# Moving work between the stages of a four-layer attention kernel: q of the linear layers, v of the second one, constants, and the order on each engine

## The chip, the cores and the metric

The kernel runs on one core of one Trainium2 chip. The profile lists its engines apart: TensorE (PE) for matrix products, with weight loads as PEld; VectorE (DVE); ScalarE (ACT); GpSimd (POOL); and SyncE (SP), which issues the DMAs here. They run side by side: before, PE, DVE, ACT and POOL are busy 445.8, 415.8, 389.4 and 59.1 us of one span of 532.9. The metric is device time in microseconds (us). The profile is one execution of the same program; its span is about 2 us shorter than the time of that execution (532.9 of 534.6 us before).

## The reference, cut to what matters

Four layers in a row on x of 2048 tokens by 512: linear attention (A), sliding-window attention (B), A again, B again, all with 32 heads of 16. The two A layers share weights, and so do the two B layers.

```
x = x + A(norm(x)); x = x + B(norm(x)); x = x + A(norm(x)); x = x + B(norm(x))

A:  q, k, v = x @ wqkv ;  phi(t) = where(t > 0, t + 1, exp(t)) + 1e-6
    kv = sum over all tokens of phi(k) v ;  z = sum over all tokens of phi(k)
    o = (phi(q) kv) / (phi(q) z + 1e-6) ;  o @ wo
B:  q, k, v = x @ wqkv ;  softmax(q k / 4) over the last 256 tokens ;  p v ;  o @ wo
```

Two things decide the shape of the program. In A, every output token needs `kv` and `z`, which need k and v of all tokens, so each A layer is a barrier. But q of a token is needed only when that token's output is made. In B the softmax needs one exp for each score in the window, a large fixed load for ACT (the 512 exps took it 305.9 us before).

Of the kernel before, what the change touches and what calls it, by code (L numbers as in the profile page):

```python
# [10 lines left out]
P = 128  # L11
D = 512
# [10 lines left out]
    cap_s=6, cap_d=2, cap_e=6, mode=100, sem=35, k_pv=0.669, k_wo=0.738, k_next=1.117, k_q=2.69, k_ao=4.2, k_kv=2.62, k_v=0.435, ring_x=3, pe_first=4, pe_last=1,  # L23
# [63 lines left out]
def schedule(g, par):  # L87
# [39 lines left out]
    while done < len(ops):  # L127
# [6 lines left out]
        while pending and pending[0][0] <= t:  # L134
            _, i = heapq.heappop(pending)
            for e in ops[i].engs:
                heapq.heappush(ready[e], (ops[i].key, i))
# [5 lines left out]
        for e in engines:  # L143
# [3 lines left out]
            pick = None  # L147
            while ready[e]:
# [8 lines left out]
                if need:  # L157
                    if any(used[c] + m > cap[c] for c, m in need.items()) or pick_banks(banks, held, need) is None:
                        back.append((k, i))
                        continue  # L160
                pick = o
# [125 lines left out]
class Plan:  # L287


    def __init__(self, par):  # L290
        self.par = par
        self.g = Graph()
        self.build()
# [27 lines left out]
    def setup(self):  # L321
# [30 lines left out]
        pool("c3", zero(lambda: K.bmask, 1.0), 1, 200, wr=[("bmask",)])  # L352
        pool("c4", lambda e: e.affine_select(out=K.bmask[:], in_=K.bmask[:], compare_op=ALU.is_ge, fill=0.0, base=0, pattern=[[-16, 8], [0, 16]], channel_multiplier=1), 2, 300, rd=[("bmask",)], wr=[("bmask",)])
        pool("c5", lambda e: e.affine_select(out=K.bmask[:], in_=K.bmask[:], compare_op=ALU.is_ge, fill=0.0, base=15, pattern=[[16, 8], [0, 16]], channel_multiplier=-1), 3, 300, rd=[("bmask",)], wr=[("bmask",)])

        pool("c6", zero(lambda: K.hot, 1.0), 4, 200, wr=[("hot",)])
        pool("c7", lambda e: e.affine_select(out=K.hot[:], in_=K.hot[:], compare_op=ALU.is_ge, fill=0.0, base=0, pattern=[[128, 4], [-16, 32]], channel_multiplier=1), 5, 300, rd=[("hot",)], wr=[("hot",)])
        pool("c8", lambda e: e.affine_select(out=K.hot[:], in_=K.hot[:], compare_op=ALU.is_ge, fill=0.0, base=15, pattern=[[-128, 4], [16, 32]], channel_multiplier=-1), 6, 300, rd=[("hot",)], wr=[("hot",)])
        pool("c9", zero(lambda: K.spread), 7, 2000, wr=[("spread",)])
        for tg in range(4):  # L360
            pool("c10", lambda e, tg=tg: e.affine_select(out=K.spread[:, tg, :, :], in_=K.spread[:, tg, :, :], compare_op=ALU.not_equal, fill=1.0, base=-32 * tg, pattern=[[-8, 4], [-1, 8], [0, 16]], channel_multiplier=1), 8, 700, rd=[("spread",)], wr=[("spread",)])
        pool("c11", zero(lambda: K.eps), 9, 100, wr=[("eps",)])
        pool("c12", lambda e: e.memset(K.eps[0:1, :], EPS_HI), 10, 100, rd=[("eps",)], wr=[("eps",)])
        pool("c13", lambda e: e.memset(K.eps[32:33, :], EPS_LO), 10, 100, rd=[("eps",)], wr=[("eps",)])

        pool("c14", zero(lambda: K.tri, 1.0), 11, 200, wr=[("tri",)])
        sel = lambda i, base, pat, cm: (lambda e: e.affine_select(out=K.tri[:, i, :], in_=K.tri[:, i, :], compare_op=ALU.is_ge, fill=0.0, base=base, pattern=pat, channel_multiplier=cm))
        pool("c15", sel(0, 0, [[1, 64]], -1), 12, 200, rd=[("tri",)], wr=[("tri",)])
        pool("c15", sel(1, 64, [[1, 64]], -1), 12, 200, rd=[("tri",)], wr=[("tri",)])
        pool("c15", sel(1, -64, [[0, 64]], 1), 12, 200, rd=[("tri",)], wr=[("tri",)])  # L370
# [3 lines left out]
        pool("c17", lambda e: e.iota(K.row[:], pattern=[[0, 1]], base=0, channel_multiplier=1), 13, 150, wr=[("row",)])  # L374
# [4 lines left out]
        for s in range(4):  # L379
            pool("c21", lambda e, s=s: e.memset(K.vB[:, s, :, :, :], 0.0), 17, 1100, wr=[("vB", s)])  # L380
            pool("c22", lambda e, s=s: e.memset(K.vB[0:64, s, :, :, 16:17], 1.0), 18, 130, rd=[("vB", s)], wr=[("vB", s)])
            pool("c23", lambda e, s=s: e.memset(K.vB[64:128, s, :, :, 33:34], 1.0), 18, 130, rd=[("vB", s)], wr=[("vB", s)])

        for q in range(2):
            for k in range(4):
                pool("wp", lambda e, q=q, k=k: e.tensor_copy(
                    K.wBp[:, q, k, :].rearrange("p (r a d) -> p r a d", a=2, d=DH),
                    K.nat(512 * q, 512 * q + 512)[:, k, :].rearrange("p (a r d) -> p r a d", a=2, d=DH)), 20 + q, 700,
                    rd=[("wBn",)], wr=[("wBp", q, k)])
        for s in range(3):  # L390
            pool("c24", lambda e, s=s: e.memset(K.pb[:, s, :, :, 320:384], 0.0), 30, 1000,
# [65 lines left out]
    def phi(self, ps, out, wr, key):  # L457
        K = self
        s = self.n_phi = getattr(self, "n_phi", -1) + 1
        s %= 3  # L460
# [4 lines left out]
    def a_k(self, t, key):  # L465
# [3 lines left out]
        self.phi(ps, lambda: K.pk[:, t, :], [("pk", t)], key + 0.1)  # L469
# [7 lines left out]
    def a_q(self, t, key):  # L477
        K = self
        ps = self.feat("q", t, lambda c, f: K.wA[:, c, f * P:(f + 1) * P], lambda c: K.XQ[:, c, t * P:(t + 1) * P], [("XQ", t), ("wAq",)], key)
        self.phi(ps, lambda: K.XQ[:, :, t * P:(t + 1) * P], [("XQ", t)], key + 0.1)  # L480

    def a_kv(self, t, kv, z, key):
# [12 lines left out]
        self.pe("kv", put, key, 4, 128, occ=330, rd=[("pk", t), ("vA", t), ("ones",)], ps=[kv, z])  # L495

    def layer_a_keys(self, ph, base):
        self.cls = "E"
        for t in range(T):
# [4 lines left out]
            self.a_q(t, k + 1.0)  # L504

    def barrier(self, ph):
# [3 lines left out]
        kv, z = Tile(1, "K", late), Tile(1, "K", late)  # L510
        key = 100 * ph + 16
        for t in range(T):
            self.a_kv(t, kv, z, key + 1.7 + t * 0.001 if late else 100 * ph + t + 0.6)
        key += 2
        if late:
            for t in range(T):
                self.a_q(t, key + t * 0.05)
# [321 lines left out]
```

## The kernel before: the parts that the change touches

The program is not written in its final order. Python code lists operations with a priority key (small is early), the engines that may do them, and what they read and write. A greedy list scheduler with estimated durations then fixes the order on each engine. At each moment an engine takes the ready operation with the smallest key whose PSUM banks are free. So a key is only a wish: an operation with a late key still runs early if its engine would otherwise idle.

```python
PAR = dict(cap_s=6, cap_d=2, cap_e=6, ..., k_pv=0.669, k_wo=0.738, k_next=1.117, k_q=2.69, k_ao=4.2, ...)

# the choice, once per engine and moment (cut)
while ready[e]:
    k, i = heapq.heappop(ready[e]); o = ops[i]
    ...
    if need:      # PSUM banks that this operation has to take first
        if any(used[c] + m > cap[c] for c, m in need.items()) or pick_banks(banks, held, need) is None:
            back.append((k, i))
            continue                     # and go on to the next key
    pick = o
    break
```

Constants (masks, selectors, zeros) are built by GpSimd with keys 1 to 30. The norms come at keys from 100, and their power `rs = (var + eps) ** -0.5` runs on GpSimd too.

```python
pool("c9", zero(lambda: K.spread), 7, 2000, wr=[("spread",)])     # one of some 40 like it
...
def layer_a_keys(self, ph, base):                # first A layer
    for t in range(T):                           # T = 16 tiles of 128 tokens
        k = 100 * ph + t
        self.norm(t, k - 0.5, ...)
        self.a_k(t, k)
        self.a_v(t, k + 0.05)
        self.a_q(t, k + 1.0)                     # q right behind k and v

def barrier(self, ph):                           # end of an A layer
    ...                                          # sums kv and z; if late (second A layer): key of a_kv is key + 1.7
    if late:
        for t in range(T):
            self.a_q(t, key + t * 0.05)          # all q of the second A layer, in plain order
    ...                                          # M = kv @ wo, denominators, reciprocals

def middle(self, ph):                            # a B layer, with A's output in front of it
    ...
    for j in range(T):                           # a "step": 8 score groups, 16 exps, 4 value groups
        ...                                      # front of tile j + 3: A's output, norm, B's q and k
        for f in range(4):
            for b in range(2):
                self.b_scores(j, f, b, base + j + (2 * f + b) / 8)
            ...                                  # b_values
        ...                                      # B's output, next norm
        self.a_k(j, k + 0.2)                     # second A layer's k and v of the same tile
        self.a_v(j, k + 0.3)
```

A score group is four matmuls into four PSUM banks, followed by two exps. A step has eight such groups.

The softmax here doesn't subtract the row's maximum and nothing guards it: scores larger than these inputs give would overflow.

## Time and profile before

The time before is 535.9 us (median of 4 runs, 534.8 to 537.3). I cut the span into stages at events that the trace shows: first matmul, last matmul of the first `kv` and `z`, first exp of the second layer, first exp of its twelfth step, its last exp, and first and last exp of the last layer.

| stage | before, us |
|---|---|
| start, to the first matmul | 21.6 |
| keys of the first A layer | 54.9 |
| first barrier, to the first exp | 22.2 |
| second layer, 11 steps | 138.7 |
| second layer, rest, to its last exp | 59.5 |
| second barrier, to the next first exp | 49.2 |
| last layer, first to last exp | 178.8 |
| end | 8.0 |

The windows view of the kernel before gives each engine's busy time (and instruction count) in roughly these stretches, then the granted PE clock, the DMA share and GB/s:

```profile
core 0: us, PE busy (x) PEld busy (x) DVE busy (x) ACT busy (x) POOL busy (x), PEclk, DMA share, GB/s
0.00:22.00 22.00, 0.44 (x4) 0.35 (x4) 7.79 (x31) 1.28 (x1) 18.45 (x44) 1.00 0.88 286
22.00:76.00 54.00, 52.64 (x566) 35.14 (x564) 42.12 (x102) 35.71 (x62) 13.69 (x23) 1.00 0.01 2
76.00:99.00 23.00, 16.79 (x258) 11.34 (x256) 18.79 (x38) 7.80 (x16) 2.19 (x4) 1.00 0.01 2
99.00:237.00 138.00, 126.51 (x1996) 77.21 (x1996) 123.53 (x300) 122.37 (x204) 11.47 (x21) 0.99 0.18 31
237.00:297.00 60.00, 52.37 (x869) 31.46 (x868) 42.36 (x113) 47.55 (x92) 3.38 (x7) 0.89 0.14 26
297.00:346.00 49.00, 42.05 (x667) 32.87 (x667) 37.59 (x81) 17.82 (x33) 2.91 (x6) 0.97 0.02 4
346.00:525.00 179.00, 151.82 (x2740) 99.84 (x2738) 142.01 (x326) 156.32 (x266) 6.97 (x12) 0.92 0.14 32
```

Read it by stage. In the start it is mostly GpSimd that works (18.45 of 22 us; DVE 7.79, PE 0.44). In the keys PE is busy 97% of the time. In the first eleven steps of the second layer PE, DVE and ACT all stand near 90% (126.51, 123.53 and 122.37 of 138 us), so no engine is "the" limit. In the last layer they stand at 85, 79 and 87%.

The timeline of GpSimd before shows why PE starts so late. The last constants run until 20.4, and `rs` only then. In the same trace DVE had the first `ve`, which `rs` reads, at 4.8 us:

```profile
17.85 0.52 POOL L382 MEMSET vB<- 64x32 bf16 x2
18.43 1.97 POOL L391 MEMSET pb<- 128x1024 bf16 x2
20.48 5.10 POOL L402 TENSOR_TENSOR rs<-ve,negh 128x1 f32<-128x1 f32 x8
```

So in this trace `rs`, with its input ready, waited some 15.7 us (20.48 less 4.8) behind constants that nobody needed yet.

### The profile page before, as it was taken

What the parts mean: (1) busy time and instruction counts of PE and PEld (TensorE: products, weight loads), DVE (VectorE), ACT (ScalarE), POOL (GpSimd) and SP (SyncE); (2) the same over time, 40 slices, a digit from 0 to 9 for tenths busy, and PEclk for the clock granted to TensorE, in tenths of its full rate; (3) what the DMA queues carried; (4) which work ended last, traced back from release to release, by engine and by line L of the source; (5) the groups of instructions that cost most, each with busy time, mean ns of one, the idle gap of its engine ahead of it and who ended that gap; (6) DMA issues with size and microseconds to landing.
All of it is one profiled execution on the core that took longest, in us unless ns stands there. A gap on an engine that the chain in (4) does not pass through costs nothing.

```text
span 532.9 us, 16311 instructions
## 1 busy us (share of the span) xinstructions
PE 445.8 (84%) x7124; PEld 289.6 (54%) x7124; DVE 415.8 (78%) x988; ACT 389.4 (73%) x673; POOL 59.1 (11%) x114
## 2 busy tenths in 40 slices
PE   0399987888999999999877997888998989787676
PEld 0156754644655556566444675655555656555443
DVE  4497769788988899999765759899799889777543
ACT  0166762689988889899886343389799889899962
POOL 8860001001000010000000000100000000000000
PEclk9999999989999999999887999899899999999756
DMA  8500000011221111121111000002121111121001
GB/s 276 197 2 1 2 2 2 1 31 31 32 33 31 32 31 32 33 35 38 32 22 21 12 1 2 1 12 42 25 47 31 33 42 33 32 50 33 21 22 31
DMA packets 45767, 18.48 MB, mean 35 GB/s; under 512 B 38016, under 2 KB 45184, under 8 KB 45696
## 3 DMA queue, kind: packets, MB, share of 16 engines
q1 hardware_dynamic: 45696, 17.44, 14.3%
q8 instruction: 56, 0.92, 0.7%
q14 instruction: 15, 0.12, 0.1%
HBM read 6.29 MB, written 2.10 MB: 16 GB/s over the span
## 4 chain that ended last, share of the span: by engine, by line
PE 45%; DVE 30%; ACT 14%; DMA 5%; POOL 4%; issue 2%; POOLq 0%; DVEq 0%
PE ps L438 14%; ACT pb L624 10%; PE ps L452 10%; PE ps L652 9%; DVE xres L565 5%; PE ps L612 5%; DVE pb L632 4%; PE ps L592 3%; DVE vB L427 3%; DVE kB L579 3%; DVE stats L399 3%; DMA oT<-o 3%; DMA XQ<-xn 2%; DVE pqd L559 2%; DVE XQ L463 2%
## 5 line engine op out<-in xcount | busy, mean ns | idle before, releaser
L624 ACT ACTIVATE pb<-ps 128x640 bf16<-128x640 f32 (+4 forms) x512 | 305.9, 675 | 33.1 <-PE ps L612 30.2
L632 DVE TENSOR_TENSOR pb<-pb,tri 128x512 bf16<-128x512 bf16 x224 | 92.7, 415 | 16.4 <-ACT pb L624 15.0
L612 PE MATMUL ps<-XQ,kB 32*128 32x320 bf16 (+4 forms) x1024 | 80.7, 305 | 26.5 <-ACT pb L624 24.9
L652 PE MATMUL ps<-vB,pb 128*128 128x34 bf16 x2880 | 90.6, 179 | 4.9 <-DVE xres L565 2.0
L652 PEld LDWEIGHTS ps<-vB,pb 128*128 128x128 bf16 x2880 | 80.8, 97 | 18.8 <-DVE xres L565 3.9
L402 POOL TENSOR_TENSOR rs<-ve,negh 128x1 f32<-128x1 f32 x64 | 35.9, 561 | 391.7 <-DVE ve L401 378.7
L612 PEld LDWEIGHTS ps<-XQ,kB 32*128 32x128 bf16 x1024 | 26.0, 91 | 86.1 <-ACT pb L624 70.7
L452 PE MATMUL ps<-xT,wBp 128*128 128x128 bf16 x1024 | 69.5, 221 | 3.0 <-DVE kB L579 0.9
L438 PE MATMUL ps<-wA,XQ 128*128 128x512 bf16 x256 | 67.0, 395 | 4.4 <-DMA XQ<-xn 2.8
L461 ACT ACTIVATE tE<-ps 128x512 bf16<-128x512 f32 x64 | 38.0, 597 | 37.7 <-PE ps L438 19.0
L452 PEld LDWEIGHTS ps<-xT,wBp 128*128 128x128 bf16 x1024 | 58.3, 98 | 12.2 <-DVE kB L579 1.2
L565 DVE TENSOR_TENSOR xres<-ps,xres 128x512 bf16<-128x512 f32 x64 | 43.8, 686 | 12.3 <-PE ps L438 11.8
L399 DVE BATCH_NORM_STATS2 stats<-xres 128x6 f32<-128x512 bf16 x64 | 43.1, 683 | 3.3 <-DMA xres<-in_A_x_dram 3.1
L579 DVE TENSOR_TENSOR kB<-ps,half 128x1024 bf16<-128x1024 f32 x32 | 39.1, 1221 | 6.8 <-PE ps L452 6.6
L438 PE MATMUL ps<-wBo,oT 128*128 128x512 bf16 x128 | 35.9, 402 | 6.6 <-DMA oT<-o 2.9
L438 PE MATMUL ps<-M,pqd 128*128 128x512 bf16 x128 | 36.0, 403 | 4.6 <-DVE pqd L559 2.7
L592 PE MATMUL ps<-wBv,xT 128*64 128x256 bf16 x512 | 37.3, 293 | 1.4 <-DVE o L665 0.2
L427 DVE CAST vB<-ps 64x512 bf16<-64x512 f32 x42 | 29.1, 694 | 11.1 <-ACT vB L427 8.8
L438 PEld LDWEIGHTS ps<-wA,XQ 128*128 128x128 bf16 x256 | 21.9, 100 | 29.0 <-issue 3.8
L462 DVE TENSOR_SCALAR tE<-tE 128x512 bf16<-128x512 bf16 x64 | 20.1, 314 | 20.4 <-ACT tE L461 20.3
L452 PE MATMUL ps<-XQ,wA 128*128 128x128 bf16 x512 | 33.0, 219 | 1.3 <-DVE XQ L463 0.9
L403 DVE TENSOR_SCALAR xn<-xres,mv,rs 128x512 bf16<-128x512 bf16 x64 | 25.9, 407 | 8.3 <-POOL rs L402 8.1
(77 smaller groups left out, 410.2 us busy)
## 6 DMA issues: line engine op xcount, KB each, us to landing
out_dram<-xres SPq DMA_DIRECT2D x16, 128.0 KB, 1.7
wA<-in_A_wqkv_dram SPq DMA_DIRECT2D x3, 512.0 KB, 6.2
xres<-in_A_x_dram SPq DMA_DIRECT2D x2, 512.0 KB, 8.8
pb<-in_B_wqkv_dram SPq DMA_DIRECT2D x1, 1024.0 KB, 9.8
xres<-in_A_x_dram SPq DMA_DIRECT2D x3, 256.0 KB, 5.4
wAo<-in_A_wo_dram SPq DMA_DIRECT2D x1, 512.0 KB, 8.4
wBv<-in_B_wqkv_dram SPq DMA_DIRECT2D x1, 512.0 KB, 9.9
wBo<-in_B_wo_dram SPq DMA_DIRECT2D x1, 512.0 KB, 9.9
```

The costliest lines, as they stand in the source:

```text
L399: self.on("DVE", "stats", lambda e: e.bn_stats(K.stats[:, t, :], K.xres[:, t, :]), key, dve(512), rd=[("xres", t)], wr=[("stats", t)])
L427: return self.either(name, lambda e, eng: e.activation(out(), src(), ACT.Copy) if eng == "ACT" else e.tensor_copy(out(), src()), key, n, r ...
L438: m = e.matmul(K.ps(ps), lhs(c), rhs(c), start=c == 0, stop=c == 3)
L452: m = e.matmul(K.ps(ps)[:, f * P:(f + 1) * P], w(c, f), xT(c), start=c == 0, stop=c == 3)
L461: self.on("ACT", "E", lambda e: e.activation(K.tE[:, s, :], K.ps(ps), ACT.Exp, bias=0.0), key, act(512), wr=[("tE", s)], ps=[ps])
L565: self.on("DVE", "res", lambda e: e.tensor_tensor(K.xres[:, t, :], K.ps(po), K.xres[:, t, :], ALU.add), key, dve(512), rd=[("xres", t)], w ...
L579: self.on("DVE", "bke", lambda e: e.tensor_tensor(K.kB[:, r, :, :, :], K.ps(pk).rearrange("p (b n) -> p b n", b=8).unsqueeze(2).to_broadca ...
L592: m = e.matmul(K.ps(pv)[64 * a:64 * a + 64, 256 * b:256 * b + 256], K.xT[:, s, c, 64 * b:64 * b + 64], K.wBv[:, c, 256 * a:256 * a + 256], ...
L612: m = e.matmul(K.ps(ps[gq])[:, 0:n], K.kB[rows, j % 4, 2 * f + b, :, :], K.XQ[rows, f, 64 * blk:64 * blk + n], start=True, stop=True, tile ...
L624: return e.activation(K.pb[:, sl, f, g0:g1 + 1, o:o + n], K.PS[:, b0:b1 + 1:b1 - b0, 0:n], ACT.Exp, bias=0.0, scale=0.25)
L632: return e.tensor_tensor(x, x, K.tri[:].unsqueeze(1).to_broadcast([P, 4, 2, 64]), ALU.mult)
L652: m = e.matmul(K.ps(ps)[:, 34 * u:34 * u + 34], K.pb[:, (b // 2) % 3, f, gq, o:o + P], K.vB[:, (b // 2) % 4, b % 2, r, :], start=i == 0, s ...
```

## The change

The intent is to fill idle time by moving work: q of the A layers is made near the step that reads it, v of the second A layer fills idle TensorE time, constants stand behind the first norms, and each B layer gets keys of its own. A rule is added to the scheduler (below, "hold rule"): while a score group waits for banks that are about to come free, other TensorE work may not take banks. No arithmetic changes.

```diff
-    cap_s=6, ..., k_pv=0.669, k_wo=0.738, k_next=1.117, k_q=2.69, ...
+    cap_s=8, ..., wait_s=400, k_aq2=8.74, k_aq3=-1.1, k_akv=14.0, k_pv2=0.299, k_wo2=0.304, ..., k_av2=17.96, k_ak2=0.155, ..., k_pv3=0.527, ...
@@ the scheduler
                         back.append((k, i))
+                        if "S" in need:
+                            n = sum(1 for x in giving if x[0] <= t + par["wait_s"])
+                            held_back = held_back or len(banks) + n >= 4
                         continue
+                if held_back and o.end is None and e == "PE" and any(x.banks is None for x in o.tiles):
+                    back.append((k, i))
+                    continue
@@ constants: all but four keys + 150
-        pool("c9", zero(lambda: K.spread), 7, 2000, wr=[("spread",)])
+        pool("c9", zero(lambda: K.spread), 157, 2000, wr=[("spread",)])
@@ first A layer
-            self.a_q(t, k + 1.0)
+            self.a_q(t, 200 + 4 * (t // 4) + 0.2 * (t % 4) - self.par["k_aq2"])
@@ second A layer
-            self.a_kv(t, kv, z, key + 1.7 + t * 0.001 if late else ...)
+            self.a_kv(t, kv, z, 100 * ph + self.par["k_akv"] + t * 0.001 if late else ...)
-                self.a_q(t, key + t * 0.05)
+                self.a_q(t, 300 + 4 * (t // 4) + 0.2 * (t % 4) - self.par["k_aq3"])
@@ in each step of the second layer
-                self.a_k(j, k + 0.2)
-                self.a_v(j, k + 0.3)
+                self.a_k(j, k + par["k_ak"])
+                self.a_v(j, base + par["k_av"] + 0.01 * j)
```

(Cut: the other constants, which move in the same way; a temporary ring split in two; `a_kv` of the late sum waits for the last value group; in each B layer TensorE transposes two tiles fewer, which DMA transposes instead.)

More of the change, by code (lines that the diff above doesn't have):

```diff
@@ L22 @@
 PAR = dict(
-    cap_s=6, cap_d=2, cap_e=6, mode=100, sem=35, k_pv=0.669, k_wo=0.738, k_next=1.117, k_q=2.69, k_ao=4.2, k_kv=2.62, k_v=0.435, ring_x=3, pe_first=4, pe_last=1,
+    cap_s=8, cap_d=2, cap_e=6, mode=100, sem=35, ring_x=3, wait_s=400, act_bias=0.0, k_aq2=8.74, k_aq3=-1.1, k_akv=14.0, k_pv2=0.299, k_wo2=0.304, k_next2=1.1, k_q2=2.637, k_ao2=4.213, k_kv2=2.52, k_v2=0.435, k_av2=17.96, k_ak2=0.155, pe_first2=2, pe_last2=1, k_pv3=0.527, k_wo3=1.163, k_next3=1.814, k_q3=2.809, k_ao3=3.596, k_kv3=2.792, k_v3=0.497, pe_first3=2, pe_last3=1,
 )
@@ L136, in schedule @@
             for e in ops[i].engs:
-                heapq.heappush(ready[e], (ops[i].key, i))
+                k = ops[i].key
+                if e == "ACT" and len(ops[i].engs) > 1:
+                    k += par["act_bias"]
+                heapq.heappush(ready[e], (k, i))
         while giving and giving[0][0] <= t:
@@ L147, in schedule @@
             pick = None
+            held_back = False
             while ready[e]:
@@ L292, in __init__ @@
         self.g = Graph()
+        self.n_phi = [0, 0]
+        self.closing = []
         self.build()
@@ L350, in setup @@
         pool("c2b", zero(lambda: K.ones, 1.0), key + 2, 150, wr=[("ones",)])
-        pool("c3", zero(lambda: K.bmask, 1.0), 1, 200, wr=[("bmask",)])
-        pool("c4", lambda e: e.affine_select(out=K.bmask[:], in_=K.bmask[:], compare_op=ALU.is_ge, fill=0.0, base=0, pattern=[[-16, 8], [0, 16]], channel_multiplier=1), 2, 300, rd=[("bmask",)], wr=[("bmask",)])
-        pool("c5", lambda e: e.affine_select(out=K.bmask[:], in_=K.bmask[:], compare_op=ALU.is_ge, fill=0.0, base=15, pattern=[[16, 8], [0, 16]], channel_multiplier=-1), 3, 300, rd=[("bmask",)], wr=[("bmask",)])
@@ L356, in setup @@
-        pool("c6", zero(lambda: K.hot, 1.0), 4, 200, wr=[("hot",)])
-        pool("c7", lambda e: e.affine_select(out=K.hot[:], in_=K.hot[:], compare_op=ALU.is_ge, fill=0.0, base=0, pattern=[[128, 4], [-16, 32]], channel_multiplier=1), 5, 300, rd=[("hot",)], wr=[("hot",)])
-        pool("c8", lambda e: e.affine_select(out=K.hot[:], in_=K.hot[:], compare_op=ALU.is_ge, fill=0.0, base=15, pattern=[[-128, 4], [16, 32]], channel_multiplier=-1), 6, 300, rd=[("hot",)], wr=[("hot",)])
-        pool("c9", zero(lambda: K.spread), 7, 2000, wr=[("spread",)])
@@ L360, in setup @@
-        for tg in range(4):
-            pool("c10", lambda e, tg=tg: e.affine_select(out=K.spread[:, tg, :, :], in_=K.spread[:, tg, :, :], compare_op=ALU.not_equal, fill=1.0, base=-32 * tg, pattern=[[-8, 4], [-1, 8], [0, 16]], channel_multiplier=1), 8, 700, rd=[("spread",)], wr=[("spread",)])
-        pool("c11", zero(lambda: K.eps), 9, 100, wr=[("eps",)])
-        pool("c12", lambda e: e.memset(K.eps[0:1, :], EPS_HI), 10, 100, rd=[("eps",)], wr=[("eps",)])
-        pool("c13", lambda e: e.memset(K.eps[32:33, :], EPS_LO), 10, 100, rd=[("eps",)], wr=[("eps",)])
@@ L366, in setup @@
-        pool("c14", zero(lambda: K.tri, 1.0), 11, 200, wr=[("tri",)])
+        pool("c3", zero(lambda: K.bmask, 1.0), 151, 200, wr=[("bmask",)])
+        pool("c4", lambda e: e.affine_select(out=K.bmask[:], in_=K.bmask[:], compare_op=ALU.is_ge, fill=0.0, base=0, pattern=[[-16, 8], [0, 16]], channel_multiplier=1), 152, 300, rd=[("bmask",)], wr=[("bmask",)])
+        pool("c5", lambda e: e.affine_select(out=K.bmask[:], in_=K.bmask[:], compare_op=ALU.is_ge, fill=0.0, base=15, pattern=[[16, 8], [0, 16]], channel_multiplier=-1), 153, 300, rd=[("bmask",)], wr=[("bmask",)])
@@ new lines, in setup @@
+        pool("c6", zero(lambda: K.hot, 1.0), 154, 200, wr=[("hot",)])
+        pool("c7", lambda e: e.affine_select(out=K.hot[:], in_=K.hot[:], compare_op=ALU.is_ge, fill=0.0, base=0, pattern=[[128, 4], [-16, 32]], channel_multiplier=1), 155, 300, rd=[("hot",)], wr=[("hot",)])
+        pool("c8", lambda e: e.affine_select(out=K.hot[:], in_=K.hot[:], compare_op=ALU.is_ge, fill=0.0, base=15, pattern=[[-128, 4], [16, 32]], channel_multiplier=-1), 156, 300, rd=[("hot",)], wr=[("hot",)])
+        pool("c9", zero(lambda: K.spread), 157, 2000, wr=[("spread",)])
@@ new lines, in setup @@
+        for tg in range(4):
+            pool("c10", lambda e, tg=tg: e.affine_select(out=K.spread[:, tg, :, :], in_=K.spread[:, tg, :, :], compare_op=ALU.not_equal, fill=1.0, base=-32 * tg, pattern=[[-8, 4], [-1, 8], [0, 16]], channel_multiplier=1), 158, 700, rd=[("spread",)], wr=[("spread",)])
+        pool("c11", zero(lambda: K.eps), 159, 100, wr=[("eps",)])
+        pool("c12", lambda e: e.memset(K.eps[0:1, :], EPS_HI), 160, 100, rd=[("eps",)], wr=[("eps",)])
+        pool("c13", lambda e: e.memset(K.eps[32:33, :], EPS_LO), 160, 100, rd=[("eps",)], wr=[("eps",)])
@@ L367, in setup @@
+        pool("c14", zero(lambda: K.tri, 1.0), 161, 200, wr=[("tri",)])
         sel = lambda i, base, pat, cm: (lambda e: e.affine_select(out=K.tri[:, i, :], in_=K.tri[:, i, :], compare_op=ALU.is_ge, fill=0.0, base=base, pattern=pat, channel_multiplier=cm))
-        pool("c15", sel(0, 0, [[1, 64]], -1), 12, 200, rd=[("tri",)], wr=[("tri",)])
-        pool("c15", sel(1, 64, [[1, 64]], -1), 12, 200, rd=[("tri",)], wr=[("tri",)])
-        pool("c15", sel(1, -64, [[0, 64]], 1), 12, 200, rd=[("tri",)], wr=[("tri",)])
+        pool("c15", sel(0, 0, [[1, 64]], -1), 162, 200, rd=[("tri",)], wr=[("tri",)])
@@ L371, in setup @@
+        pool("c15", sel(1, 64, [[1, 64]], -1), 162, 200, rd=[("tri",)], wr=[("tri",)])
+        pool("c15", sel(1, -64, [[0, 64]], 1), 162, 200, rd=[("tri",)], wr=[("tri",)])
         self.on("DVE", "c16", lambda e: e.tensor_tensor(K.tri[:, 0, :], K.tri[:, 0, :], K.tri[:, 1, :], ALU.add), 12, (120, 200), rd=[("tri",)], wr=[("tri",)])
         self.on("DVE", "c16", lambda e: e.tensor_scalar(K.tri[:, 1, :], K.tri[:, 0, :], -1.0, 1.0, op0=ALU.mult, op1=ALU.add), 12, (120, 200), rd=[("tri",)], wr=[("tri",)])
-        pool("c17", lambda e: e.iota(K.row[:], pattern=[[0, 1]], base=0, channel_multiplier=1), 13, 150, wr=[("row",)])
+        pool("c17", lambda e: e.iota(K.row[:], pattern=[[0, 1]], base=0, channel_multiplier=1), 163, 150, wr=[("row",)])
@@ L379, in setup @@
         for s in range(4):
-            pool("c21", lambda e, s=s: e.memset(K.vB[:, s, :, :, :], 0.0), 17, 1100, wr=[("vB", s)])
-            pool("c22", lambda e, s=s: e.memset(K.vB[0:64, s, :, :, 16:17], 1.0), 18, 130, rd=[("vB", s)], wr=[("vB", s)])
-            pool("c23", lambda e, s=s: e.memset(K.vB[64:128, s, :, :, 33:34], 1.0), 18, 130, rd=[("vB", s)], wr=[("vB", s)])
+            pool("c21", lambda e, s=s: e.memset(K.vB[:, s, :, :, :], 0.0), 167, 1100, wr=[("vB", s)])
+            pool("c22", lambda e, s=s: e.memset(K.vB[0:64, s, :, :, 16:17], 1.0), 168, 130, rd=[("vB", s)], wr=[("vB", s)])
+            pool("c23", lambda e, s=s: e.memset(K.vB[64:128, s, :, :, 33:34], 1.0), 168, 130, rd=[("vB", s)], wr=[("vB", s)])
         for q in range(2):
@@ L387, in setup @@
                     K.wBp[:, q, k, :].rearrange("p (r a d) -> p r a d", a=2, d=DH),
-                    K.nat(512 * q, 512 * q + 512)[:, k, :].rearrange("p (a r d) -> p r a d", a=2, d=DH)), 20 + q, 700,
+                    K.nat(512 * q, 512 * q + 512)[:, k, :].rearrange("p (a r d) -> p r a d", a=2, d=DH)), 170 + q, 700,
                     rd=[("wBn",)], wr=[("wBp", q, k)])
         for s in range(3):
-            pool("c24", lambda e, s=s: e.memset(K.pb[:, s, :, :, 320:384], 0.0), 30, 1000,
+            pool("c24", lambda e, s=s: e.memset(K.pb[:, s, :, :, 320:384], 0.0), 180, 1000,
                  rd=[("wBp", q, k) for q in range(2) for k in range(4)] if s == 2 else [],
@@ L455, in feat, with phi @@
         return ps
-    def phi(self, ps, out, wr, key):
+    def phi(self, ps, out, wr, key, ring):
         K = self
-        s = self.n_phi = getattr(self, "n_phi", -1) + 1
-        s %= 3
+        n = self.n_phi[ring] = self.n_phi[ring] + 1
+        s = 2 * ring + n % 2
         self.on("ACT", "E", lambda e: e.activation(K.tE[:, s, :], K.ps(ps), ACT.Exp, bias=0.0), key, act(512), wr=[("tE", s)], ps=[ps])
@@ L468, in a_k @@
         ps = self.tok("k", t, xT, lambda c: K.wA[:, c, 512:1024], [("XQ", t), ("wAk",)], key)
-        self.phi(ps, lambda: K.pk[:, t, :], [("pk", t)], key + 0.1)
+        self.phi(ps, lambda: K.pk[:, t, :], [("pk", t)], key + 0.1, 0)
     def a_v(self, t, key):
@@ L479, in a_q @@
         ps = self.feat("q", t, lambda c, f: K.wA[:, c, f * P:(f + 1) * P], lambda c: K.XQ[:, c, t * P:(t + 1) * P], [("XQ", t), ("wAq",)], key)
-        self.phi(ps, lambda: K.XQ[:, :, t * P:(t + 1) * P], [("XQ", t)], key + 0.1)
+        self.phi(ps, lambda: K.XQ[:, :, t * P:(t + 1) * P], [("XQ", t)], key + 0.1, 1)
     def a_kv(self, t, kv, z, key):
@@ L493, in put @@
             return m
-        self.pe("kv", put, key, 4, 128, occ=330, rd=[("pk", t), ("vA", t), ("ones",)], ps=[kv, z])
+        self.pe("kv", put, key, 4, 128, occ=330, rd=[("pk", t), ("vA", t), ("ones",)], ps=[kv, z], after=self.closing)
     def layer_a_keys(self, ph, base):
@@ L509, in barrier @@
         late = ph == 2
-        kv, z = Tile(1, "K", late), Tile(1, "K", late)
+        kv, z = Tile(1, "K", False), Tile(1, "K", False)
         key = 100 * ph + 16
         for t in range(T):
-            self.a_kv(t, kv, z, key + 1.7 + t * 0.001 if late else 100 * ph + t + 0.6)
+            self.a_kv(t, kv, z, 100 * ph + self.par["k_akv"] + t * 0.001 if late else 100 * ph + t + 0.6)
         key += 2
@@ L565, in resid, with b_qkv @@
         self.on("DVE", "res", lambda e: e.tensor_tensor(K.xres[:, t, :], K.ps(po), K.xres[:, t, :], ALU.add), key, dve(512), rd=[("xres", t)], wr=[("xres", t)], ps=[po])
-    def b_qkv(self, t, s, key):
+    def b_qkv(self, t, s, key, key2):
         K = self
-        par = self.par
         rd = [("xT", s)]
@@ L575, in b_qkv @@
         self.copy("bqe", ps, lambda: K.XQ[:, :, t * P:(t + 1) * P], lambda ps=ps: K.ps(ps).rearrange("p (f n) -> p f n", f=4), key + 0.05, 512, wr=[("XQ", t)])
-        key += par["k_q"] - par["k_kv"]
+        key = key2
         pk = self.feat("bk", t, lambda c, f: K.wBp[:, 1, c, f * P:(f + 1) * P], xT, rd + wk, key)
@@ L679, in middle @@
         K.cls = "D"
-        par = self.par
+        par = {k[:-1]: v for k, v in self.par.items() if k[-1] == str(ph)}
+        par["ring_x"] = self.par["ring_x"]
         base = 100 * ph
@@ L688, in front @@
             self.a_out(t, k - par["k_ao"])
-            self.norm(t, k - par["k_ao"] + 0.3, t % ring, lambda: K.xT[:, t % ring, :, :], [("xT", t % ring)], t < par.get("pe_first", 3))
-            self.b_qkv(t, t % ring, k - par["k_q"])
+            self.norm(t, k - par["k_ao"] + 0.3, t % ring, lambda: K.xT[:, t % ring, :, :], [("xT", t % ring)], t < par["pe_first"])
+            self.b_qkv(t, t % ring, k - par["k_q"], k - par["k_kv"])
         for t in range(min(3, T)):
@@ L705, in middle @@
                     self.b_values(j, h, base + j + (h + 1) / 2 + par["k_pv"])
+            if not last:
+                self.closing = [self.g.ops[-1]]
             k = base + j + 1 + par["k_wo"]
-            tail = j >= T - par.get("pe_last", 2)
+            tail = j >= T - par["pe_last"]
             self.b_out(j, k, tail)
@@ L746, in run @@
             sb("pk", [T, D]); sb("vA", [T, D]); sb("kB", [4, 8, 2, 64]); sb("vB", [4, 2, 16, 34]); sb("pb", [3, 4, 4, 704])
-            sb("o", [2, D]); sb("oT", [2, 4, P]); sb("rc", [2, 2, 16], F32); sb("tE", [3, D])
+            sb("o", [2, D]); sb("oT", [2, 4, P]); sb("rc", [2, 2, 16], F32); sb("tE", [4, D])
             sb("stats", [T, 6], F32); sb("mv", [T, 2], F32); sb("ve", [T, 1], F32); sb("rs", [T, 1], F32)
```

## The prediction

> **What bounds the kernel now.** The limit changes by stage. I cut the span (532.9 us) with the windows view at the first matmul, the end of the first keys, and the first and last exp of each sliding layer:
>
> - start, 0 to 22: PE 0.4 us busy. The timeline shows why: GpSimd builds constants until 20.5 and only then computes the norms' `rs` (a power), although the first `ve` was ready at 4.8.
> - first keys, 22 to 76: PE busy 52.6 of 54, so PE-bound; per tile q takes 0.89, k and v 1.75, all about 3.2.
> - first barrier, 76 to 98: PE 16, DVE 18.2, ACT 7 of 22.
> - second layer, 98 to 291: steps of 12.5; PE, DVE, ACT each 85 to 95% busy. Exps alone about 150.
> - second barrier, 291 to 346: ACT about 40% busy; 14 tiles of q (12.5 of PE) run here.
> - last layer, 346 to 533: ACT 84%, steps 11.3; the last 33 us at about half the clock.
>
> **What the change does.** The arithmetic stays; orders move. From the compared orders:
>
> 1. Constants: the first two `rs` now stand behind the 1.8 us memset of `spread` (ends 5.9), so near 7.2, not 21.6. PE starts near 7.5 to 9 (key weights land about 8.5). Later `rs` alternate with constants: by GpSimd's durations tiles 2-3 near 11.5, 4-5 near 18, 6-7 near 20.5, 8-12 at 25 to 28. That just feeds PE at 2.3 per tile. Gain 14 us.
> 2. First q: 5 of 32 halves stay among the keys, which drop to about 2.3 a tile (DVE then needs as much), ending near 50. But 25 halves run before the first scores, so the barrier grows from 22 to about 28: each q adds about 0.95 of DVE. First exp near 80 instead of 98.7: 18 to 20 with point 1, less 2 for q in the first steps.
> 3. v of the second linear layer: 0.88 of PE and 0.6 of evacuation leave each steady step; 24 of 32 halves go to the last steps, whose exps leave PE room, 8 to the barrier. Scores stand evenly between other matmuls, all 8 PSUM banks usable. Steps fall to about 11.7; gain 8.
> 4. Second barrier: 26 q halves, not 28, but 4 more v halves; fewer q before the denominators: gain 3.
> 5. Last layer: own keys, even scores; ACT needs 10.1 for exps plus half the copies, 10.9 against 11.3: gain 6.
>
> All of it is on the critical path: 33 to 37 us less some loss. [...] the first eight 512-wide matmuls took 3.24, later ones 1.75. [...]
>
> **Prediction: 502 us**, 8 in 10 between 490 and 516. Chances: faster by over 2% 0.95, within 2% 0.04, slower 0.01.
>
> **What would show it.** (1) first matmul near 8; (2) keys ending near 50, first exp near 80, DVE over 90% busy between; (3) steps near 11.7, v late in the layer, PE busier there; (4) last exp of the second layer to first of the next near 52; (5) last layer about 181 with ACT at 87%.
>
> **What would make it wrong.** GpSimd starving the keys between 12 and 25; DVE giving back in the barrier all that PE gains; scores in eight banks starving the two-bank work, so that steps stay at 12.5; v in the tail delaying scores; a lower granted clock.

The sum: the terms come to 33 to 37 us off 535.9, which gives 499 to 503, plus a loss of 1 to 2 us for a start whose matmuls run slowly for longer, so 500 to 505; 502 was put down. The trace of before shows the slow first matmuls alone: the first eight with 512 columns took 3.24 us (at 22.86), eight later ones 1.89 in the same view (at 41.63), or 1.73 from their start to that of the next matmul. The "about half the clock" of the last 33 us reads 0.55 in the windows view (500 to 533).

## More of the kernel before

The waits view of ACT in the steady steps (before, 174 to 237 us) shows the exps waiting for scores, and the exp of k's phi (`tE`) waiting for k's matmuls: total us, times, longest.

```profile
ACT pb L624 <- PE ps L612: 3.7, 10, 0.5
ACT tE L461 <- PE ps L438: 2.3, 5, 1.0
```

In each of five steps of 12.6 us that is 0.7 us for scores, and 1.2 us in all.

## The result, and the profile after

The changed kernel takes 494.9 us (median of 4 runs, 492.2 to 496.7). The ratio to the kernel before is 0.923, with a 95% interval of 0.918 to 0.928. Ratios here are the mean time of one kernel's fast runs over that of the other's of the same rounds, so not quite the ratio of the medians. Executions over 1.5% slower than the fastest of the same kernel are left out of the means. Where I give a ratio as microseconds, I multiply by 536.

| stage | before | after | difference | predicted |
|---|---|---|---|---|
| start | 21.6 | 7.2 | -14.4 | -14 |
| keys | 54.9 | 47.6 | -7.3 | about -12 |
| first barrier | 22.2 | 24.9 | +2.7 | +6 |
| second layer, 11 steps | 138.7 | 135.6 | -3.1 | -6 with the rest |
| second layer, rest | 59.5 | 56.6 | -2.9 | |
| second barrier | 49.2 | 41.5 | -7.7 | -3 |
| last layer and end | 186.8 | 179.7 | -7.1 | -6 |
| span | 532.9 | 493.1 | -39.8 | -33 to -37, less a loss |

The same view of the kernel after, cut at its own stage ends:

```profile
core 0: us, PE busy (x) PEld busy (x) DVE busy (x) ACT busy (x) POOL busy (x), PEclk, DMA share, GB/s
0.00:7.00 7.00, 0.00 (x0) 0.00 (x0) 2.53 (x8) 1.28 (x1) 5.38 (x18) 1.00 0.68 202
7.00:55.00 48.00, 44.81 (x378) 24.87 (x384) 37.81 (x108) 24.86 (x43) 27.83 (x49) 1.00 0.31 103
55.00:80.00 25.00, 21.97 (x349) 18.32 (x350) 24.53 (x55) 10.31 (x19) 2.19 (x4) 1.00 0.03 8
80.00:215.00 135.00, 117.99 (x2030) 77.88 (x2049) 121.19 (x297) 123.82 (x212) 10.97 (x21) 0.97 0.19 32
215.00:272.00 57.00, 53.66 (x899) 33.45 (x908) 47.10 (x118) 50.32 (x98) 3.38 (x6) 1.00 0.14 28
272.00:313.00 41.00, 38.41 (x628) 30.82 (x632) 31.82 (x75) 18.61 (x34) 3.29 (x6) 1.00 0.08 11
313.00:485.00 172.00, 145.42 (x2711) 99.03 (x2732) 138.01 (x322) 157.52 (x269) 6.59 (x12) 0.93 0.15 33
```

The first barrier has become DVE-bound (24.53 of 25 us): q's phi runs there. In the tail of the second layer PE is busy 53.66 of 57 us with v and q. The GpSimd timeline answers to the one of before:

```profile
4.11 1.80 POOL L357 MEMSET spread<- 128x2048 bf16 x1
5.97 0.12 POOL L357 MEMSET eps<- 128x32 bf16 x1
6.18 1.18 POOL L414 TENSOR_TENSOR rs<-ve,negh 128x1 f32<-128x1 f32 x2
7.51 1.01 POOL L373 TENSOR_SCALAR_AFFINE_SELECT spread<-spread 128x512 bf16<-128x512 bf16 x1
```

The first two `rs` now run at 6.18, and the remaining constants fill in behind. ACT's wait for scores in six steady steps after (144 to 215 us) is this line, again about 0.75 us a step; the wait for k's matmuls has nearly gone (0.2 us in all six):

```profile
ACT pb L635 <- PE ps L623: 4.5, 6, 0.8
```

The first part of the page gives PE before and after, in us and instructions:

```profile
PE 445.8 (84%) x7124; PEld 289.6 (54%) x7124; DVE 415.8 (78%) x988; ACT 389.4 (73%) x673; POOL 59.1 (11%) x114
```

```profile
PE 426.4 (86%) x7038; PEld 286.8 (58%) x7108; DVE 405.5 (82%) x982; ACT 387.4 (79%) x675; POOL 59.6 (12%) x114
```

Matmuls were "busy" 19.4 us less, while weight loads changed by 2.8 us. Of the 86 matmuls fewer, 16 are transposes that the change took from TensorE (there are 16 weight loads fewer as well); the other 70 (1%) are missing records, all of 512 columns, at some 0.22 us each, about 15 us of the 19.4.

The granted clock changed as well. Its mean is 0.950 before and 0.964 after; the records show half clock for 53 and 36 us. If TensorE set the pace in all of that difference, it would be worth some 9 us of the 39.8 (an estimate: half of 53 less 36). What of it comes from the new order, and what from chance, is not separated.

### The profile page after: what moved, and what is told of

It is laid out like the page before. It is cut to its first block, busy times and chain, and to the rows that moved or that the text cites. A ratio compares the mean times of both kernels' runs of the same rounds, so it can differ in the third digit from the quotient of the medians.

```text
span 493.1 us, 16212 instructions
## 1 busy us (share of the span) xinstructions
PE 426.4 (86%) x7038; PEld 286.8 (58%) x7108; DVE 405.5 (82%) x982; ACT 387.4 (79%) x675; POOL 59.6 (12%) x114
## 4 chain that ended last, share of the span: by engine, by line
PE 39%; ACT 28%; DVE 23%; DMA 3%; POOL 3%; issue 2%; POOLq 0%
ACT pb L635 22%; PE ps L450 11%; PE ps L663 10%; PE ps L464 10%; PE ps L623 6%; DVE pb L643 3%; DVE xres L577 3%; DVE stats L411 2%; DVE pk L475 2%; ACT vB L439 2%; DVE tE L474 2%; ACT tE L473 2%; DVE pqd L571 2%; DVE XQ L475 2%; DMA XQ<-xn 2%
## 5 line engine op out<-in xcount | busy, mean ns | idle before, releaser
L663 PE MATMUL ps<-vB,pb 128*128 128x34 bf16 x2880 | 84.7, 179 | 3.7 <-ACT pb L635 1.3
L663 PEld LDWEIGHTS ps<-vB,pb 128*128 128x128 bf16 x2880 | 77.9, 97 | 13.8 <-ACT pb L635 2.7
L450 PE MATMUL ps<-wA,XQ 128*128 128x512 bf16 x232 | 61.3, 396 | 5.8 <-DVE pb L643 1.3
L464 PEld LDWEIGHTS ps<-xT,wBp 128*128 128x128 bf16 x1024 | 59.3, 100 | 11.5 <-DVE kB L590 1.5
L473 ACT ACTIVATE tE<-ps 128x512 bf16<-128x512 f32 x64 | 38.1, 597 | 27.4 <-PE ps L464 12.4
L450 PE MATMUL ps<-wBo,oT 128*128 128x512 bf16 x111 | 31.6, 404 | 7.5 <-DMA oT<-o 2.0
L464 PE MATMUL ps<-XQ,wA 128*128 128x128 bf16 x512 | 35.0, 219 | 0.3 <-DVE recf L554 0.2
L603 PE MATMUL ps<-wBv,xT 128*64 128x256 bf16 x512 | 34.9, 280 | 0.0
L450 PE MATMUL ps<-M,pqd 128*128 128x512 bf16 x101 | 28.6, 388 | 4.6 <-issue 1.5
L464 PEld LDWEIGHTS ps<-XQ,wA 128*128 128x128 bf16 x512 | 30.1, 98 | 4.1 <-DVE recf L554 0.4
```

Of the source, the lines that this page charges most:

```text
L450: m = e.matmul(K.ps(ps), lhs(c), rhs(c), start=c == 0, stop=c == 3)
L464: m = e.matmul(K.ps(ps)[:, f * P:(f + 1) * P], w(c, f), xT(c), start=c == 0, stop=c == 3)
L473: self.on("ACT", "E", lambda e: e.activation(K.tE[:, s, :], K.ps(ps), ACT.Exp, bias=0.0), key, act(512), wr=[("tE", s)], ps=[ps])
L603: m = e.matmul(K.ps(pv)[64 * a:64 * a + 64, 256 * b:256 * b + 256], K.xT[:, s, c, 64 * b:64 * b + 64], K.wBv[:, c, 256 * a:256 * a + 256], ...
L663: m = e.matmul(K.ps(ps)[:, 34 * u:34 * u + 34], K.pb[:, (b // 2) % 3, f, gq, o:o + P], K.vB[:, (b // 2) % 4, b % 2, r, :], start=i == 0, s ...
```

## The experiments

Twelve kernels ran, all correct, three rounds each, beside the kernel before on the same chip. Names with `b_` are the kernel before with one part of the change; those with `a_` are the changed kernel with one part undone or altered; `q_norm9` builds on `a_qearly_even`. "Steady step" is the mean of the sixth to the eleventh step of the second layer, from the ACT records of the trace (before: 12.7 us, after: 11.9 us).

| kernel | median us | ratio to before | steady step | last layer, exps |
|---|---|---|---|---|
| before | 535.9 | 1 | 12.7 | 178.8 |
| after | 494.9 | 0.923 | 11.9 | 171.6 |
| b_const | 525.6 | 0.982 | 12.8 | 179.3 |
| b_vlate | 530.7 | 0.989 | 12.6 | 180.9 |
| b_hold | 524.9 | 0.980 | 12.9 | 169.6 |
| b_holdvlate | 524.0 | 0.979 | 13.1 | 169.2 |
| a_constearly | 506.1 | 0.945 | 11.9 | 174.3 |
| a_qearly | 506.8 | 0.947 | 12.6 | 174.3 |
| a_qearly_even | 494.8 | 0.923 | 11.8 | 170.1 |
| a_vearlyq | 507.3 | 0.948 | 13.3 | 170.4 |
| a_q3flat | 497.9 | 0.928 | 11.8 | 167.5 |
| a_nohold (3 fast runs) | 518.0 | 0.962 | 13.1 | 174.8 |
| a_norm9 | 493.1 | 0.921 | 11.8 | 171.9 |
| q_norm9 | 496.7 | 0.926 | 11.9 | 176.2 |

A caution for all of them: one changed key lets the greedy scheduler reorder later stages as well. So I read each from the stage that the edit is about, and only then from the total. The 95% intervals of the ratios are 0.003 to 0.007 to either side (2 to 4 us); none reaches 1.

A second caution is the granted clock. From the first exp of the last layer on, a_qearly_even and q_norm9 run the same instructions in the same order on every compute engine. Yet the layer took 170.1 us in one profile and 176.2 in the other, at mean clocks of 0.95 and 0.91:

```profile
314.30:484.40 170.10, 145.06 (x2742) 99.68 (x2762) 139.80 (x327) 158.51 (x273) 6.68 (x12) 0.95 0.15 35
```

```profile
311.70:487.90 176.20, 154.02 (x2766) 101.40 (x2762) 140.02 (x327) 159.25 (x273) 6.68 (x12) 0.91 0.14 33
```

So a difference of up to 6 us in the last layer, from one profile each, need not be the edit's.

Two more readings of it, both from the changed kernel. The windows view gives 1.00 for 7 to 17 us, where eight matmuls with 512 columns took 3.60 us instead of some 1.9, so there the column does not tell how fast PE ran. And from 102 to 109 us it gives 0.51, with PE busy 6.22 of 7 us: sixteen matmuls of `xT` and `wBp` took 1.89 us there (at 106.84) and 1.07 at 109.05. Just before that stretch stands a gap of 2.0 us, in which PE waited for a transposed tile (until 100.97). That the gap is the cause is not shown.

### The constants alone, and undone

```diff
 b_const: keys c3 to c24 of the kernel before + 150      a_constearly: the same keys of the changed kernel - 150
```

> The kernel before with nothing but the constants' new keys. Theory: its first keys are bound by PE at 3.2 us a tile, so constants between the rs cost nothing there, and the whole saving at the start arrives at the end: first matmul near 7.2, end of the first keys near 63, total 536 less 12 to 14. Rival: rs starves PE between 12 and 28 us here too, and only about 7 us arrive.

> The changed kernel with the constants put back in front of the norms. Theory: the first matmul moves from 7.2 to about 21.5, but the first keys, which in the changed kernel take 47.4 us because GpSimd alternates constants and rs, then run at what DVE needs, about 2.4 us a tile, and end near 62 instead of 54.7; the loss is about 7 us of 494. Rival: the stages only add up, the keys take 47.4 us whenever they start, and the whole 14.3 us come back (about 509).

The constants alone gave 9.5 us (1 - 0.982 of 536); undoing them cost 11.6 us (0.9446 - 0.923). Both lie between theory and rival. In both pairs the start changed by the full 14.4 us and the keys gave back 4 to 5: b_const's keys took 60.0 us against 54.9, and a_constearly's 43.5 against 47.6. So the move is worth about 10 us at either end, and my first account of who absorbs what was wrong for the kernel before: its keys, though PE-bound, lost 5 us too.

Part of what is given back shows in the first matmuls with 512 columns. The timelines of PE, first the kernel after, then a_constearly:

```profile
8.53 3.60 PE L450 MATMUL ps<-wA,XQ 128*128 128x512 bf16 x8
13.64 4.34 PE L450 MATMUL ps<-wA,XQ 128*128 128x512 bf16 x12 [1.04 <-DVE XQ L434]
```

```profile
22.85 4.52 PE L450 MATMUL ps<-wA,XQ 128*128 128x512 bf16 x14
```

Later fourteen such matmuls take 3.18 us in the same view (at 23.81 in the kernel after, at 29.84 in a_constearly), about 0.22 each. Twenty of them took 7.9 us after, 3.5 us over that; fourteen took 4.5 us in a_constearly, 1.5 us over. After the early start PE runs slowly for longer, for 2 us of the difference. That its pause of 1.04 us, in which it waited for DVE, is the reason is my guess, and was not tested; in a_norm9 the pause is 0.30 us, and the twelve matmuls behind it took 3.09 us instead of 4.34. The rest of the 4 us I put down to norms that DVE had finished during the long start in a_constearly (eight `ve` were ready when `rs` began); that is argued, not tested.

### GpSimd out of the keys' way

```diff
+ for o in constants_but_the_first_four:
+     o.deps.append(rs_of_tile[9])
```

> The changed kernel with all of GpSimd's constants but the four that the norms need made to wait for rs of the tenth tile. Theory: GpSimd's alternation costs the keys about 4 us (47.6 us against 43.5 with the constants in front), so the keys end near 50 and the total falls by 3 to 5 us to about 490. Rival: DVE limits the keys anyway, or the constants come late in the barrier, and nothing is gained.

> The same on the kernel with q among the keys and the even order (a_qearly_even). Theory: its keys, 58.8 us, have a TensorE floor of about 52; without the alternation they take about 54, and the total falls from 494.8 to about 490. Rival as for a_norm9.

The rival won. In a_norm9 the first ten `rs` come sooner (the third at 8.2 us instead of 10.9, the fifth at 13.0 instead of 18.1), and the keys shrink from 47.6 to 46.4 us; the total of 493.1 us is not clear of the changed kernel's (intervals 0.916 to 0.926 and 0.918 to 0.928). q_norm9 is not faster than its base either. So my fear that GpSimd's alternation starves the keys was about three times too large: I expected 4 us in the keys, and it costs 1.2 there and 0.8 in the start.

### q of the first A layer back among the keys

```diff
-            self.a_q(t, 200 + 4 * (t // 4) + 0.2 * (t % 4) - self.par["k_aq2"])
+            self.a_q(t, k + 1.0)
```

> The changed kernel with q of the first linear layer back behind each tile's keys (keys 1.0 later, as before). Theory: the keys take about 3.2 us a tile and end near 61 instead of 54.7, but the barrier shrinks from 25 to 22 us and the first steps of the second layer lose their q: first exp near 83.5, second step shorter by 4 us, total slower by 0 to 4 us. Rival: the delay of q earns the whole fall of the keys' stage, 7.5 us or more.

The total rose by 12.9 us, which looked like the rival's victory. But the stages said otherwise. The keys grew by 11.2 us and the barrier shrank by 2.9, so the first exp came 8.3 us later; then the first two steps were 6.2 us shorter (23.3 against 29.5). That leaves 2 us. The rest of the loss sat later, where no q of this layer is left: 5.7 us in steps three to eleven (steady steps of 12.6 us instead of 11.9), 4.2 in the rest of the second layer and 2.7 in the last layer. The order of the steps had changed: B's v and the second A layer's k (1.9 us of matmuls) now stood between the same two score groups. So one more key was changed:

```diff
-    k_ak2=0.155
+    k_ak2=0.3
```

> The kernel with the early q, and one key more (k of the second linear layer 0.3 instead of 0.155 behind its norm), which brings the steady steps back to the order of the changed kernel: between two score groups no longer v and k of 1.9 us together. Theory: the early q itself costs little; its 12 us came from the order of the steady steps (12.5 us against 11.8), so the steps are 11.8 again, the total falls from 506.8 to about 497 to 499. Rival: the early q costs what it cost whatever the order, total within 2 us of 507.

The steps came back to 11.8 us and the total to 494.8 us, ratio 0.9228: the time of the changed kernel. At the first exp of the twelfth step the two stand at 216.8 and 215.3 us. This is the greater part of a step in ACT's timeline, first of a_qearly, then of a_qearly_even:

```profile
200.34 1.30 ACT L635 ACTIVATE pb<-ps 128x640 bf16<-128x640 f32 x2 [0.18 <-PE ps L623]
202.04 0.65 ACT L439 ACTIVATE vB<-ps 64x512 bf16<-64x512 f32 x1 [0.40 <-DVE vB L439]
202.71 0.60 ACT L473 ACTIVATE tE<-ps 128x512 bf16<-128x512 f32 x1
203.21 3.77 ACT L635 ACTIVATE pb<-ps 128x640 bf16<-128x640 f32 x6
207.23 2.52 ACT L635 ACTIVATE pb<-ps 128x640 bf16<-128x640 f32 x4 [0.26 <-PE ps L623]
```

```profile
198.42 0.59 ACT L439 ACTIVATE vB<-ps 64x512 bf16<-64x512 f32 x1
198.90 0.70 ACT L635 ACTIVATE pb<-ps 128x640 bf16<-128x640 f32 x1
199.48 0.60 ACT L473 ACTIVATE tE<-ps 128x512 bf16<-128x512 f32 x1
199.96 3.07 ACT L635 ACTIVATE pb<-ps 128x640 bf16<-128x640 f32 x5
203.80 1.92 ACT L635 ACTIVATE pb<-ps 128x640 bf16<-128x640 f32 x3 [0.77 <-PE ps L623]
```

In the first, ACT stops several times (the brackets are its idle time and what ended it); in the second it runs from 192.6 to 203 without a pause and stops once. The bracketed idle time is about the same, 0.84 and 0.77 us. Over five steps ACT was idle 1.0 and 0.8 us a step, and busy 11.6 and 11.0 us with the same instructions. So most of the difference is no wait that the view shows, and its cause stays open. The one key also moved `spread` and value groups, so it isn't shown either that v and k in one gap were the fault.

Two conclusions follow. Putting off q of the first A layer earned nothing in the total: what the keys save comes back in the barrier and the first steps. (The late q with the key 0.3 was not run.) And the order, a matter of one key, is worth some 12 us in the timed runs. By the profiles 6.2 lie in the first eleven steps, 5.1 in the rest of the layer, and 4.2 in the last layer, where the clock differed too (0.91 and 0.95).

### v of the second A layer back in the steps; v alone

```diff
 a_vearlyq:
-                self.a_v(j, base + par["k_av"] + 0.01 * j)
+                self.a_v(j, k + 0.3)
                 # and q of the second A layer waits for a score group of step 14, its place in the changed kernel
 b_vlate:
-                self.a_v(j, k + 0.3)
+                self.a_v(j, base + 17.96 + 0.01 * j)
```

> The changed kernel with v of the second linear layer back in each step, and its q kept from moving forward in turn (they wait for a score of step 14, where they begin in the changed kernel). Theory: steady steps of the second layer go from 11.8 to about 12.4 us (7 us over the layer), and the tail loses its filling work, so the records show half clock there again and the stretch from the twelfth step to the first exp of the last layer falls by less than the v work that left it. Total slower by 4 to 8 us. Rival: the even order of scores alone makes the steps 11.8, they stay so, and the total is the same within 2 us.

> The kernel before with nothing changed but the key of v in the second linear layer (last, so it fills idle TensorE time). Theory, as in the prediction: each steady step loses 0.88 us of PE and 0.6 of evacuation, so steps fall from 12.5 to about 11.8, and the tail takes v up at no cost: faster by 5 to 8 us. Rival: v helps only together with the even order; the steps stay over 12.3 and the gain is under 3 us.

Putting v back cost 13.3 us, more than expected: steps rose to 13.3 us, above those of before. The tail and the second barrier together did not shrink although some 8 us of v left them (100.7 us against 98.1; v of 9 of the 16 tiles, at 0.88 us), so there v had been free. But the steps' order changed with v: up to 2.8 us of other matmuls stand between two score groups, against 1.7 in the changed kernel, and PE was busy only 69.40 of 80 us. Whether another key would give an even order with v in the step, as it did for a_qearly, was not run.

v alone, in b_vlate, left the steps at 12.6 us. It gained 6.1 us in the timed runs (ratio 0.989). Its one profile gained 3.9, spread over the early steps, the tail and the barrier, less 2.1 lost in the last layer.

The windows view of steady steps shows what became of the freed time: five of before, six of b_vlate, six of after.

```profile
174.00:237.00 63.00, 59.70 (x976) 36.90 (x976) 57.18 (x140) 56.84 (x95) 5.24 (x10) 1.00 0.20 33
```

```profile
158.00:234.00 76.00, 65.63 (x1165) 43.68 (x1167) 67.07 (x170) 67.72 (x109) 6.58 (x12) 1.00 0.17 33
```

```profile
144.00:215.00 71.00, 63.78 (x1140) 42.29 (x1149) 65.10 (x162) 66.29 (x115) 6.19 (x13) 1.00 0.21 36
```

Before, PE is busy 95% of the step, 11.9 us of it. Without v PE falls to 86% and ACT stands at 89%: nobody is full, and PE's freed time turned into idle time. The wait of exps for scores rose from 0.7 to 1.2 us a step; the wait for k's matmuls is gone, so ACT waits 1.2 us in all, as before:

```profile
ACT pb L624 <- PE ps L612: 7.2, 14, 0.7
```

Only in the order of the changed kernel does ACT reach 93% and the step 11.9 us; ACT then waits 0.8 us a step.

Late v on its own also goes with a higher clock in the rest of the layer. Before, the granted clock was 0.89 there (0.50 from 285 to 290 us); in b_vlate it is 1.00, with v's work added for PE:

```profile
233.90:291.90 58.00, 52.48 (x886) 32.20 (x892) 44.46 (x119) 49.33 (x95) 3.56 (x7) 1.00 0.16 27
```

It is 0.88 to 0.91 in the four kernels with v in the steps (before, b_const, b_hold, a_vearlyq), and 1.00 in all with late v but a_nohold (0.95).

### The hold rule: undone, alone, and with v

```diff
 a_nohold:
-                            held_back = held_back or len(banks) + n >= 4
+                            held_back = False
 b_hold, b_holdvlate: the rule, with 400 ns, added to before and to b_vlate
```

> The changed kernel with the rule taken out that holds other TensorE work back while a score group waits for banks. Theory: the even order of the steps comes from this rule; without it two matmul groups come between scores again, steps of the second layer go to 12.3 or more and of the last to 11.2, total slower by 8 to 12 us. Rival: v's leaving alone made the steps shorter, and they stay at 11.8 and 10.8.

> The kernel before with nothing added but the rule that holds other TensorE work back while a score group waits for banks; v stays in each step. Theory: the rule and the departure of v belong together. With v in the step, the evenly ordered gaps are too full (here k and two value groups stand in one gap, about 2.2 us against 1.26 us of exps), so steps stay between 12.3 and 13.3 and the total is within 1.5% of before. Rival: the rule earns alone what its removal cost, 15 us or more.

> The kernel before with both the hold rule and v put last. Theory: the two together shorten the steps of the second layer to about 12.0 (one gap still holds k and two value groups, so not quite 11.8), faster by 8 to 14 us than before, more than the sum of b_vlate and b_hold. Rival: they add up or cancel, 3 to 7 us.

Taking the rule away cost 20.9 us, the most of any part. Its profile, of a run of 520.9 us, has 10.1 more in the first 11 steps of the second layer, 12.4 in its rest, where late v and q now stand in front of scores (three steps take 16 to 17 us), and 3.2 in the last layer. Adding the rule to the kernel before gained 10.8 us, of which 9.2 lie in the last layer (169.6 us against 178.8) and none in the steady steps of the second (12.9). So on the kernel before, the rule shortens the last layer: three profiles without it have 178.8 to 180.9 us, two with it 169.6 and 169.2. The clock goes with it (0.92 and 0.95), so part of this may be the clock's. In the changed kernel the 3.2 us lie within the 6.1 us by which two profiles of one order differ, at clocks of 0.95 and 0.91. The rule together with late v gained 11.3, no more than the rule alone, and its steps were 13.1 us, not the 12.0 that I expected. So "rule plus v" is not what makes 11.9 either; something else of the change is needed too, most likely the keys that were found for the second layer, which were not run alone. In the changed kernel's order, `bv s k*2 s bout*2 s spread pv*2 s aout*2 s bq*2 s pv*2 s bk*2 s` (s is a score group), no gap holds more than 1.7 us of other matmuls. In b_holdvlate one gap holds two value groups and k, 2.2 us. But b_vlate has no gap over 1.7 us either, and steps of 12.6. So the largest gap alone is not the law, and which features an order must have stays open.

### q of the second A layer in plain order

```diff
-                self.a_q(t, 300 + 4 * (t // 4) + 0.2 * (t % 4) - self.par["k_aq3"])
+                self.a_q(t, key + t * 0.05)
```

> The changed kernel with q of the second linear layer in plain order as before, so that q of later tiles stands in front of the denominators in the second barrier. Theory: that is what made the barrier before 49.2 us (10 halves of q between M and the first denominator, 6.6 us on the chain); here M to the first denominator takes 2 to 6 us longer and the barrier 44 to 47 instead of 41.5; total slower by 3 to 5 us. Rival: the barrier gained by v's filling work and the full clock, and stays within 1 us of 41.5.

The barrier grew from 41.5 to 46.5 us, as the theory said. DVE's timelines show the path from M to the denominators' reciprocal, for before, after and a_q3flat in turn:

```profile
317.74 1.28 DVE L427 CAST M<-ps 128x512 bf16<-128x512 f32 x2
...
324.37 0.95 DVE L542 RECIPROCAL recf<-ps 128x128 f32<-128x128 f32 x1
```

```profile
292.82 0.68 DVE L439 CAST M<-ps 128x512 bf16<-128x512 f32 x1
...
293.62 0.95 DVE L554 RECIPROCAL recf<-ps 128x128 f32<-128x128 f32 x1
```

```profile
292.21 0.68 DVE L439 CAST M<-ps 128x512 bf16<-128x512 f32 x1
...
295.18 0.95 DVE L554 RECIPROCAL recf<-ps 128x128 f32<-128x128 f32 x1
```

The first reciprocal comes 6.6, 0.8 and 3.0 us after M. That is 2.2 of the 5.0 us; behind the reciprocal, too, the critical chain of a_q3flat goes through q's phi on DVE (four times between 296 and 300 us). Yet the last layer of a_q3flat is 4.1 us shorter (167.5), and the profiled span is 492.7 against 493.1. That its q is done by then is one reason; the clock, 0.95 in that layer against 0.93, is a rival. The timed runs give 0.928 against 0.923 with overlapping intervals. So a net gain of some 3 us from this q is possible and not shown.

## Why the prediction was right

The total, 494.9 us, lies inside 490 to 516. It was a sum of terms, and they did not all hold.

- **The constants and the start** (14 us at the start) held: first matmul at 7.2. At the end of the kernel the move is worth about 10, as b_const and a_constearly show. A start whose matmuls run slowly for longer, as I had warned, is there: 2 us (twenty matmuls took 3.5 us over their later pace, against 1.5 for fourteen in a_constearly). The later `rs` came up to 5 us later than I had put them (tiles 8 to 12 at 27 to 33 us, predicted 25 to 28), and they were hardly a bottleneck: a_norm9, where they come sooner, is faster by 1 to 2 us at most.
- **First q**: I expected the keys to end near 50 and the barrier to take 28 us; they ended at 54.7 and it took 24.9, so the first exp came at 79.7, as predicted (80). The two errors cancelled, so that hit was luck. DVE was over 90% busy in the barrier (98%) but not in the keys (79%). I gave the first steps a loss of 2 us; against the early q it was 6.2. The net of this q is zero (a_qearly_even), where my figures left 2 to 4 us.
- **v**: the size held (steps 11.9, predicted 11.7), the reason did not. The step that failed is "0.88 of PE and 0.6 of evacuation leave each steady step ... Steps fall to about 11.7". In b_vlate the work left and the steps stayed at 12.6. Among the kernels with late v the steps range from 11.8 to 13.1 with the order; which feature of the order does it stays open. That v's leaving makes room is argued: a step with v has 11.9 us of PE work (before), so a step of 11.9 would leave PE no pause. a_vearlyq, 13.3 with v back, can't decide it, as its order changed too. "All 8 PSUM banks usable" played no part in it: with `cap_s=6` the built order on PE is the same for the first 935 of 967 operations, so it could touch only the very end. This was compared as built, not run.
- **Second barrier**: mis-sized, 3 us predicted and 7.7 measured. I had noted "fewer q before the denominators" without sizing the DVE chain behind it; a_q3flat puts 5.0 us back. The other 2.7 us I did not test. On the total this gain may count less: in a_q3flat the last layer was 4.1 us shorter, and the clock may have its share in that.
- **Last layer**: 6 predicted, 7.1 measured with the end. On the kernel before, the hold rule, and with it the even scores, gives 9.2 us here (b_hold), part of which may be the clock's. The layer's own keys were not isolated; with them and without the rule the layer takes 174.8 us, 4.0 less than before, which is within the 6.1 us by which two profiles of one order differ.

The parts don't add to the whole: alone on the kernel before, the constants gave 9.5, late v 6.1 and the rule 10.8 us, 26 of the 41; the keys found for the two B layers were not run alone, so part of the rest may be theirs. Undone in the changed kernel, constants, v and the rule cost 11.6, 13.3 and 20.9, 46 us. Parts that only pay together are undervalued by the first test and counted twice by the second.

No version that is clear of the changed kernel's time was found; a_norm9 at 493.1 us is the lowest, within the noise.

## What to carry to other kernels

When several engines are near full, taking work out of a step shortens it only if the order lets the next engine use the freed time (in b_vlate PE fell from 95 to 86% of a step, and the step stayed at 12.6 us), so check after the removal whether any engine has become full. When one change to a priority slows later stages that hold none of the moved work, look at their order before you blame the move: here one more key turned a loss of 12 us into none. Judge a delay of work by the stage that receives it as well: q left the first stage at a gain of 11 us and cost 9 in the next two. And look at the granted clock of each stage before you give a few microseconds of one profile to an edit: here the same order took 170 and 176 us.
